# Clustered attention and two MoE layers on one core: first pair's halves placed by engines, arg max head by head, weight chunks loaded from the seventh row block on, 1e-9 added by ACT

## The chip, the core and the metric

One core of a Trainium2 chip runs the whole program. The metric is the device time of one execution in microseconds (us). PE is TensorE, DVE is VectorE, ACT is ScalarE, POOL is GpSimd, and SP is SyncE, which only issues transfers here. "Line 450" or L450 is a line of the kernel as the profile names it.

## What is computed

```python
q_assign = argmax(q_n @ c_n.T)        # 16 clusters for each of 8 heads
k_assign = argmax(k_n @ c_n.T)
mask = q_assign[..., :, None] == k_assign[..., None, :]
scores = where(mask, q @ k.T / sqrt(D), -1e9)
scores = scores - max(scores)
attn = exp(scores)
attn = attn / (sum(attn) + 1e-9)
x = (attn @ v) as [1536, 512]
x = leaky(x @ w_in1) @ w_out1         # d_ff 2048
out = ratio(x @ w_in2) @ w_out2       # ratio of polynomials
```

Batch 2, heads 8, sequence 768, head width 64. All in float32. The weights arrive as 64-bit floats, which the kernel takes as pairs of 32-bit words.

## The kernel before

**Attention.** The 16 (batch, head) slices are taken two at a time as 8 pairs. A pair has 12 row blocks of 128 queries (six for each of its two heads), so there are 96 row blocks, called rows from here on: row 0 is the first, row 12 the first of the second pair. `run` is one loop over rows, and all engines execute what it emits in the order in which it is written. In turn i it emits the row maximum `nm` of row i (DVE), the reciprocal and the scaling of `e` for rows i-2 and i-1 (DVE, POOL), the six transposes `pT` of row i-4 (PE) with their copies `ph` (ACT) and `pl` (DVE), the exponential `e` of row i (ACT), the scores `s` of row i+1 (PE), and matmuls with the values, `o`. So each row follows row by row through PE, DVE, ACT and POOL, four turns deep.

**Float32 in two parts.** PE multiplies in a shorter format, so each operand is split into a high part and the remainder, the low part. For the scores, `a` holds for a head the high part of q over its low part (64 partitions each) and for k the low part over the high part, and `b` holds the high parts once more in its first 64 partitions, with 16 rows of one-hot cluster marks below them. A row's scores are two matmuls with `a` and two with `b`, into one tile `s`.

**Preparing a pair.** q and k are loaded (`load_qk`), transposed on PE into `pa` (`trans`), copied to `x`, split into `hl`, and moved by transfers into `a` and `b` (`place_a`, `place_b`: six transfers of 192 KB a head). For the marks, `sims` multiplies `x` with the centroids, `sims_out` copies the result to `sv`, and DVE and POOL find the first maximum and write the marks `oh` (`sims_max`, `is_max`, `rank`, `first`, `onehot`, called the arg max here); PE transposes them (`onehot_t`), ACT copies them to `ot`, and six small transfers bring them into `b` (`place_oh`). `load_v` and `vsplit` do the values. For pairs 2 to 7 a list, `plan`, says in which turn of the loop each step is emitted. For the first pair and most of the second, `startup` emits everything ahead of row 0.

**Transfers.** Nearly all are issued by SP, in the order of the code, and an issue waits until what it reads is written and what it overwrites is free.

**Weights during attention.** Four chunks of weights (512 KB each) are loaded into tiles `xst` that attention does not need yet, converted in four steps (`conv_a` on ACT, `conv_s` and two `conv_c` on DVE) and saved to DRAM. `weights.step` emits the next of these steps, and `weights.preload` emits loads. Before, two loads are emitted in `startup` ahead of the third pair's q and k, two at its end, and the steps are spread over turns 0 to 53.

**After attention** the two layers run in stages of matmuls with 384 columns (lines 900 on).

Of the kernel before, what the change touches and what calls it, by code (L numbers as in the profile page):

```python
# [17 lines left out]
P = 128  # L18
# [11 lines left out]
def clustered_attention_moe_moe2(  # L30
# [44 lines left out]
    for c in range(C):  # L75
        nc.vector.memset(iom[:, :, c:c + 1], float(c - C))
    lnb = const.tile([P, 1], F32, name="lnb")
# [52 lines left out]
    class Attention:  # L130
# [62 lines left out]
        def prep_pieces(self, p):  # L193
# [9 lines left out]
            def load_qk():  # L203
                for nm in "qk":
                    st[nm] = raw.tile([P, HP, T, D], F32, tag=f"{nm}raw", name=f"{nm}raw")
                for h in range(HP):
# [34 lines left out]
            def split_direct(h, x=True):  # L241
                new_hl(h)
                pps = [st["pp"].pop(("a", h, i)) for i in range(2)]
                if x:
                    st["x"][h] = tok.tile([P, 2, W], F32, tag="x", name="x", bufs=2)
                    for i in range(2):
                        scaled_copy(st["x"][h][:, i], i, pps[i])
                for i in range(2):
                    hi = part(h, 0, i)
                    scaled_copy(hi, i, pps[i])  # L250
                    nc.vector.scalar_tensor_tensor(
                        part(h, 1, i), pps[i], (SCALE, 1.0)[i], f32(hi),
                        op0=ALU.mult, op1=ALU.subtract,
                    )

# [51 lines left out]
            N2 = HP * NS2  # L307

            def svv():
                return st["sv"].rearrange("p h n c -> p (h n) c")  # L310

            def sims_max():
                st["mx"] = sm.tile([P, N2], F32, tag="mx", name="mx")
                nc.vector.reduce_max(st["mx"], svv(), axis=AX.X)

            def is_max():
                nc.vector.tensor_tensor(
                    svv(), svv(), st["mx"].unsqueeze(2).to_broadcast([P, N2, C]), op=ALU.is_ge
                )

            def rank(eng=gp):
                eng.tensor_tensor(svv(), svv(), iom.to_broadcast([P, N2, C]), op=ALU.mult)

            def first():
                nc.vector.tensor_reduce(st["mx"], svv(), axis=AX.X, op=ALU.min)
                st["oh"] = tok.tile([P, 2, HP, T, C], F32R, tag="oh", name="oh")

            def onehot(i):
                mx = st["mx"].rearrange("p (h i t) -> p h i t", h=HP, i=2)
                nc.vector.tensor_tensor(  # L330
                    st["oh"][:, i],
                    iom.unsqueeze(2).to_broadcast([P, HP, T, C]),
                    mx[:, :, i].unsqueeze(3).to_broadcast([P, HP, T, C]),
# [3 lines left out]
            def onehot_t(tile_=self.ptile):  # L337
                pp = tile_("po")
                st["pp"]["o"] = pp
                for i in range(2):  # L340
                    for h in range(HP):
                        j = i * HP + h
                        nc.tensor.transpose(
                            pp[0:C * T, j * P:(j + 1) * P].bitcast(F32R),
# [4 lines left out]
            def onehot_out():  # L349
                pp = st["pp"].pop("o")  # L350
                st["ot"] = tok.tile([P, 2, HP, P], F32R, tag="ot", name="ot")
                w = HP * P
                for i in range(2):
                    nc.scalar.activation(
                        st["ot"][0:C * T, i].rearrange("p h n -> p (h n)"),
                        pp[0:C * T, i * w:(i + 1) * w], AF.Copy, scale=-BIG if i == 0 else 1.0,
                    )

            def place_oh(queues=(nc.sync,)):
                for t in range(T):  # L360
                    queues[t % len(queues)].dma_start(
                        out=f32(st["b"][D:KB, :, :, t % 2 * TH + t // 2, :]),
                        in_=f32(st["ot"][t * C:(t + 1) * C]),
                    )

            def vsplit(h):
# [11 lines left out]
                load_qk, load_v, trans, trans_out, split_direct, split_hi, split_lo, place_a, place_b,  # L378
# [42 lines left out]
            if p == 1:  # L421
# [3 lines left out]
                moved = []  # L425
# [6 lines left out]
            if p == 2:  # L432
                plan = plan[1:]
# [131 lines left out]
        def startup(self, open_start, weights):  # L565
# [3 lines left out]
            self.load_centroids()  # L569
            f0["load_qk"]()  # L570
            load_consts()
            self.centroid_zero()
# [4 lines left out]

            for h in range(HP):
                halves(f0, h)
            f1["load_qk"]()  # L580
            vec.tensor_copy(identr, ident)
            for f in self.centroid_ops():
                f()
            self.centroid_t(po)
            for h in range(HP):
                f0["split_direct"](h)
                f0["place_a"](h, (nc.sync, nc.gpsimd))
                f0["place_b"](h, (nc.sync, nc.gpsimd))
            pq = lambda nm: self.pq.tile([P, 512], F32, tag="pT", name=nm)
            for h in range(HP):  # L590
                f0["sims"](h, pq)
            for h in range(HP):
                f0["sims_out"](h)
            f0["sims_max"]()
            f0["is_max"]()
            f0["rank"](vec)
# [521 lines left out]
```

## Time and profile before

| | |
|---|---|
| median of 3 runs | 841.36 us (840.57 to 842.88) |
| profiled execution, own time | 840.42 us |
| its span | 838.6 us, so 1.8 us lie around it |
| busy share | PE 95%, DVE 77%, ACT 62%, POOL 49% |
| attention, first to last row maximum | 26.55 to 276.0 us |
| transfers | 82.16 MB, mean 98 GB/s |

The busy share is an average over stages: in the two layers PE is busy nearly throughout, in the first 45 us of attention no engine is. What a change at the start is worth is read from the first 60 us, stretch by stretch.

### The profile page before, as it was taken

Reading aid. Unit: us, or ns where it says so; the run is one execution under the profiler, and the core shown is the slowest. Engines: PE = TensorE matmul, PEld = TensorE weight load, DVE = VectorE, ACT = ScalarE, POOL = GpSimd, SP = SyncE. Lnnn points to the kernel's source line nnn. Section 1 sums busy time; section 2 is a strip of 40 time slices with the busy share of each in tenths; the row PEclk is TensorE's granted clock in tenths of the full one; section 3 lists DMA queues with packets and bytes.
Section 4 is the critical chain, followed back from the end, with each engine's and each line's share of the span. In section 5 each row is a group of like instructions: output and inputs, shape, how many; then the busy total and the mean of one; then the engine's idle time right before and its main releaser. Section 6 shows DMA issues by size and latency. Waiting matters only on the chain.

```text
span 838.6 us, 13335 instructions
## 1 busy us (share of the span) xinstructions
PE 796.8 (95%) x4545; PEld 738.5 (88%) x4545; DVE 645.9 (77%) x1221; ACT 520.7 (62%) x1077; POOL 408.7 (49%) x478
## 2 busy tenths in 40 slices
PE   5689999999999899999999999998999999999997
PEld 5588888898888899999999999996889888988995
DVE  4389889889889566857466657768878888888887
ACT  3468788888888544454254345546767667766664
POOL 2676778878756522231022024256555555554442
PEclk9789999999999999999999999999999999999999
DMA  7956637637410214344545453530011110100112
GB/s 182 240 150 159 156 68 154 133 84 150 104 36 26 72 51 179 102 150 140 146 168 176 127 200 105 173 88 26 25 38 26 39 38 26 25 1 1 39 39 75
DMA packets 43987, 82.16 MB, mean 98 GB/s; under 512 B 5488, under 2 KB 26224, under 8 KB 43920
## 3 DMA queue, kind: packets, MB, share of 16 engines
q1 hardware_dynamic: 43296, 80.04, 34.2%
q0 software_dynamic: 384, 1.18, 0.6%
q8 instruction: 36, 0.59, 0.3%
q14 instruction: 31, 0.25, 0.1%
q10 hardware_dynamic: 240, 0.10, 0.1%
HBM read 50.37 MB, written 10.49 MB: 73 GB/s over the span
## 4 chain that ended last, share of the span: by engine, by line
PE 48%; POOL 20%; DVE 11%; ACT 9%; issue 8%; DMA 3%; POOLq 0%; ACTq 0%; SPq 0%; DVEq 0%
PE y L923 19%; PE h L923 19%; POOL z L975 6%; POOL z L972 4%; PE o L525 3%; DVE pl L511 3%; PE pT L492 3%; DVE nm L459 2%; PE s L450 2%; POOL wol L750 2%; ACT ln L988 2%; ACT ph L505 2%; POOL e L484 2%; POOL wil L750 2%; ACT r L989 2%
## 5 line engine op out<-in xcount | busy, mean ns | idle before, releaser
L923 PE MATMUL h<-xh,wil 128*128 128x384 f32 x512 | 172.4, 337 | 0.0
L923 PE MATMUL h<-xh,wih 128*128 128x384 f32 x512 | 172.4, 337 | 0.0
L923 PE MATMUL h<-xl,wih 128*128 128x384 f32 x512 | 172.2, 336 | 0.0
L957 DVE TENSOR_TENSOR gl<-h,gh 128x384 fp32r<-128x384 f32 x128 | 70.9, 554 | 81.2 <-ACT gh L952 64.1
L750 POOL TENSOR_TENSOR wil<-wf,wih 128x512 fp32r<-128x512 f32 x32 | 41.7, 1311 | 146.3 <-ACT wih L747 105.4
L511 DVE TENSOR_TENSOR pl<-pT,ph 128x384 fp32r<-128x384 f32 x192 | 97.1, 547 | 12.6 <-ACT ph L505 11.7
L505 ACT CAST ph<-pT 128x384 fp32r<-128x384 f32 x192 | 83.2, 485 | 33.6 <-PE pT L492 32.7
L484 POOL TENSOR_SCALAR e<-e,sum 128x768 f32<-128x768 f32 x96 | 87.6, 922 | 32.5 <-DVE sum L480 28.4
L459 DVE TENSOR_REDUCE nm<-s 128x1 f32<-128x768 f32 x96 | 91.0, 948 | 14.0 <-PE s L450 13.6
L923 PEld LDWEIGHTS h<-xh,wih 128*128 128x128 f32 x512 | 96.1, 188 | 2.6
L923 PEld LDWEIGHTS h<-xl,wih 128*128 128x128 f32 x512 | 96.0, 188 | 2.5
L470 ACT ACTIVATE e<-s,nm 128x768 f32<-128x768 f32 x96 | 87.5, 911 | 17.0 <-DVE nm L459 11.4
L923 PEld LDWEIGHTS h<-xh,wil 128*128 128x128 f32 x512 | 96.0, 187 | 0.0
L492 PE MATMUL pT<-ident,e 128*128 128x128 f32 x576 | 82.8, 278 | 11.1 <-DVE pl L511 10.8
L961 ACT ACTIVATE h<-h 128x384 f32<-128x384 f32 x64 | 30.5, 476 | 91.3 <-PE h L923 91.2
L952 ACT CAST gh<-h 128x384 fp32r<-128x384 f32 x128 | 61.7, 482 | 40.0 <-DVE h L996 37.5
L923 PE MATMUL y<-gl,woh 128*128 128x384 f32 x256 | 85.6, 334 | 0.2 <-DVE gl L957 0.2
L923 PE MATMUL y<-gh,wol 128*128 128x384 f32 x256 | 85.7, 335 | 0.0
L923 PE MATMUL y<-gh,woh 128*128 128x384 f32 x256 | 85.6, 334 | 0.0
L492 PEld LDWEIGHTS pT<-ident,e 128*128 128x128 f32 x576 | 67.7, 144 | 19.4 <-POOL sum L476 6.1
L972 POOL TENSOR_SCALAR z<-y,abv 128x384 f32<-128x384 f32 x64 | 43.5, 680 | 82.1 <-ACT y L968 82.1
L740 DVE SCALAR_TENSOR_TENSOR wf<-st,wf 128x512 int32<-128x512 int32 x120 | 82.8, 742 | 0.0
(104 smaller groups left out, 1842.1 us busy)
## 6 DMA issues: line engine op xcount, KB each, us to landing
st<-in_moe_w_in_dram SPq DMA_DIRECT2D x30, 512.0 KB, 4.6
st<-in_moe_w_out_dram SPq DMA_DIRECT2D x30, 512.0 KB, 4.5
a<-hl SPq DMA_DIRECT2D x60, 192.0 KB, 4.2
b<-hl SPq DMA_DIRECT2D x30, 192.0 KB, 6.5
wf<-scratch_wi SPq DMA_DIRECT2D x14, 256.0 KB, 3.1
wf<-scratch_wo SPq DMA_DIRECT2D x14, 256.0 KB, 2.9
qraw<-in_q_dram SPq DMA_DIRECT2D x16, 192.0 KB, 3.0
kraw<-in_k_dram SPq DMA_DIRECT2D x16, 192.0 KB, 3.3
```

The source lines that it names most:

```text
L459: nc.vector.reduce_max(un["nm"], un["s"][:, 0:S], axis=AX.X, negate=True)
L470: nc.scalar.activation(un["e"], un["s"][:, 0:S], AF.Exp, bias=un["nm"], accum_out=un["recip"])
L484: nc.gpsimd.tensor_scalar(un["e"], un["e"], un["recip"], 1.0, op0=ALU.mult, op1=ALU.mult)
L492: nc.tensor.transpose(pp[:, kt * P:(kt + 1) * P], un["e"][:, k0:k0 + P], ident)
L505: nc.scalar.copy(un["hi", part], un["pT", part])
L511: nc.vector.tensor_tensor(self.group[gi]["pl"][:, part * n:(part + 1) * n, i * P:(i + 1) * P], un["pT", part], f32(un["hi", part]), op=ALU ...
L740: nc.vector.scalar_tensor_tensor(wi, hold["st", i][:, :, :, 1 - w], sc, wi, op0=op, op1=ALU.bitwise_or)
L750: nc.gpsimd.tensor_tensor(hold["l"][:, i:i + wr, :], hold["wf", i], f32(hold["h"][:, i:i + wr, :]), op=ALU.subtract,)
L923: nc.tensor.matmul(o, lhsT=l, rhs=r, start=(first and idx == 0), stop=(last and idx == n - 1),)
L952: nc.scalar.copy(d["gh"], d["h"])
L957: nc.vector.tensor_tensor(d["gl"], d["h"], f32(d["gh"]), op=ALU.subtract)
L972: nc.gpsimd.tensor_scalar(d["z"], d["y"], abv[:, 1:2], abv[:, 0:1], op0=ALU.mult, op1=ALU.add)
```

## The change

1. In `startup` the first pair's `a` and `b` are no longer filled through `hl` and transfers. `x_out` copies both transposes to `x`; `direct` writes a high part into `a` with ACT and the low part with DVE; `direct_b` copies the high parts from `a` to `b` with POOL. Twelve transfers of 192 KB fall away.
2. The arg max of the first pair is done for each head apart, its marks too, and all its transfers are issued by SP. Before, SP and ACT issued three each.
3. `startup` loads no weights. The first call of `weights.step` is in turn 7 and emits all four loads; steps then come in two turns of three. The last transfers of the second pair's `a` and `b` are emitted in turns -1 and 0. For the third pair, transposes, copies and splits come one turn later.
4. The 1e-9 is added by ACT right behind the exponential of an odd row, and no longer by POOL at the turn's end.

```diff
-            def split_direct(h, x=True):
...
+            def x_out(h):
+                st["x"][h] = tok.tile([P, 2, W], F32, tag="x", name="x", bufs=2)
                 for i in range(2):
+                    scaled_copy(st["x"][h][:, i], i, st["pp"].pop(("a", h, i)))
+
+            def direct(h, i, u):
+                if i == 0 and u == 0:
+                    st["a"][h] = self.tr.tile([P, 2, T, P], F32R, tag="a", name="a", bufs=4)
+                src = st["x"][h][u * D:(u + 1) * D, i]
...
+                nc.scalar.copy(hi, src)
+                nc.vector.tensor_tensor(lo, src, f32(hi), op=ALU.subtract)
+
+            def direct_b(h, i):
...
+                gp.tensor_scalar(
+                    st["b"][0:D, i, h], f32(st["a"][h][i * D:(i + 1) * D, i]),
+                    1.0, 1.0, op0=ALU.mult, op1=ALU.mult,
+                )
...
-            nc.gpsimd.tensor_scalar(un["sum"], un["sum"], 1e-9, 1.0, op0=ALU.add, op1=ALU.mult)
+            nc.scalar.activation(un["sum"], un["sum"], AF.Identity, bias=eps)
...
+            split(0)
+            chain(f0, h0)
+            split(1)
+            assign(h0)
             for h in range(HP):
+                f0["vsplit"](h)
             for h in range(HP):
                 halves(f1, h)
+                by_pool(f1, h)
             f2["load_qk"]()
+            chain(f0, h1)
+            assign(h1)
+            f1["place_a"](0)
...
                     self.exp(i)
+                    if i % 2 == 1:
+                        self.denom(i)
...
-                if i % 2 == 1 and 0 <= i < NU:
-                    self.denom(i - 1)
-                if 0 <= i < NU // 2 + UP // 2:
-                    fill[1].step(2 if i % 3 == 2 else 1)
+                if UP // 2 <= i < NU - 2 * UP and i % 3:
+                    fill[1].step()
```

`split(h)` is two rounds of `direct` and `direct_b`, `chain` is the arg max of one head, `assign` its marks' transposes, copies and transfers, `by_pool` the split of the second pair.

How the instructions stand on the engines. First PE from the first `sims` to the first scores, where `pa` here is the second pair's; before:

```order
L291 MATMUL sims<-cc,x 128x32 x12
L343 MATMUL po<-identr,oh 96x128 x4
L225 MATMUL pa<-ident,qraw 128x128 x3
L225 MATMUL pa<-ident,kraw 128x128 x3
L225 MATMUL pa<-ident,qraw 128x128 x3
L225 MATMUL pa<-ident,kraw 128x128 x3
L450 MATMUL s<-a 128x512
```

and after:

```order
L307 MATMUL sims<-cc,x 128x32 x12
L365 MATMUL po<-identr,oh 96x128 x2
L230 MATMUL pa<-ident,qraw 128x128 x3
L230 MATMUL pa<-ident,kraw 128x128 x3
L230 MATMUL pa<-ident,qraw 128x128 x3
L230 MATMUL pa<-ident,kraw 128x128 x3
L365 MATMUL po<-identr,oh 96x128 x2
L477 MATMUL s<-a 128x512
```

The second head's marks now stand on PE between the second pair's transposes and row 0's scores. Next DVE in `startup`, after the change, up to the first row maximum:

```order
L262 TENSOR_TENSOR a<-x,a 64x384 x4
L335 TENSOR_REDUCE mx<-sv 128x12
L338 TENSOR_TENSOR sv<-sv,mx 128x192
L343 TENSOR_TENSOR sv<-sv,iom 128x192
L346 TENSOR_REDUCE mx<-sv 128x12
L353 TENSOR_TENSOR oh<-iom,mx 128x96 x2
L262 TENSOR_TENSOR a<-x,a 64x384 x4
L335 TENSOR_REDUCE mx<-sv 128x12
L338 TENSOR_TENSOR sv<-sv,mx 128x192
L343 TENSOR_TENSOR sv<-sv,iom 128x192
L346 TENSOR_REDUCE mx<-sv 128x12
L353 TENSOR_TENSOR oh<-iom,mx 128x96 x2
```

Before there were four subtractions (line 251, 384 wide, one input in PSUM) and then one arg max of 384 elements for both heads. Now there are eight subtractions with both inputs in SBUF and two arg maxes of half the width. Last ACT in turns 7 and 8 of the loop, after the change, from the exponential of row 7:

```order
L497 ACTIVATE e,sum<-s,nm 128x768
L503 ACTIVATE sum<-sum,eps 128x2
L767 ACTIVATE xst<-xst 128x512
L532 CAST ph<-pT 128x3x128 x2
L376 ACTIVATE ot<-po 96x256 x2
L497 ACTIVATE e,sum<-s,nm 128x768
L767 ACTIVATE xst<-xst 128x512
```

and SP around the loads that those conversions read:

```order
L220 DMA vraw<-in_v_dram 128x2x384
L286 DMA a<-hl 64x2x384 x4
L755 DMA xst<-in_moe_w_in_dram 128x2x512 x2
L755 DMA xst<-in_moe_w_out_dram 128x1024 x2
L383 DMA b<-ot 16x4x128 x6
```

Before, the conversions (L727) stood behind the exponentials of rows 0 and 1, and their loads ahead of row 0. Now the load and its conversion are emitted in the same turn, and SP has the third pair's first four transfers into `a` ahead of the load.

## Rows read from the trace of the kernel before

**Rows 1.** Stretches: length; busy PE, PEld, DVE, ACT, POOL; clock; DMA share; GB/s.

```profile
26.55:45.19 18.64, 13.53 (x70) 11.83 (x70) 9.66 (x17) 9.35 (x21) 11.12 (x15) 0.68 1.07 264
62.76:95.69 32.93, 31.04 (x211) 27.36 (x209) 31.36 (x58) 26.92 (x62) 23.51 (x31) 1.00 0.54 129
...
127.71:158.77 31.06, 30.14 (x211) 27.40 (x209) 28.00 (x52) 25.62 (x60) 24.60 (x34) 1.00 0.54 118
```

**Rows 2.** Timeline, exponentials of rows 4, 5 and 11: start, length, idle before.

```profile
38.35 0.90 ACT L470 ACTIVATE e<-s,nm 128x768 f32<-128x768 f32 x1 [0.30 <-DVE nm L459]
46.23 0.90 ACT L470 ACTIVATE e<-s,nm 128x768 f32<-128x768 f32 x1 [0.37 <-DVE nm L459]
...
61.59 0.92 ACT L470 ACTIVATE e<-s,nm 128x768 f32<-128x768 f32 x1
```

**Rows 3.** Chain that ended last, 26 to 41 us: start, length, what.

```profile
26.94 7.81 DMA a<-hl
...
39.62 0.83 POOL hl L258
```

**Rows 4.** Timeline of the start, up to row 0's scores.

```profile
6.40 0.85 PE L225 MATMUL pa<-ident,kraw 128*128 128x128 f32 x3
...
8.23 5.30 PE L291 MATMUL sims<-cc,x 128*128 128x32 f32 x24 [0.78 <-DVE cc L186]
14.51 0.56 DVE L317 TENSOR_TENSOR sv<-sv,mx 128x384 f32<-128x384 f32 x1
16.28 0.63 DVE L330 TENSOR_TENSOR oh<-iom,mx 128x192 fp32r<-128x192 f32 x2
...
25.54 0.98 PE L450 MATMUL s<-b 80*128 80x512 f32 x2 [3.77 <-DMA b<-ot]
```

**Rows 5.** Groups by line and form, 127.71 to 220.85 us: busy, mean ns.

```profile
L263 POOL TENSOR_TENSOR hl<-x,hl 128x384 fp32r<-128x384 f32 x12 | 12.0, 1009 | 0.3
L538 ACT COPY tmp<-o 64x384 f32<-64x384 f32 x12 | 5.7, 475 | 1.9 <-PE o L525 1.8
L258 POOL TENSOR_SCALAR hl<-x 128x768 fp32r<-128x768 f32 x6 | 5.0, 838 | 0.0
L476 POOL TENSOR_SCALAR sum<-sum 128x2 f32<-128x2 f32 x18 | 3.5, 192 | 5.9 <-ACT e L470 4.8
```

**Rows 6.** Timeline, DVE beside POOL, at 163 and at 44 us.

```profile
162.69 1.02 POOL L373 TENSOR_TENSOR vs<-vraw,vs 128x384 fp32r<-128x384 f32 x1
163.25 0.88 DVE L317 TENSOR_TENSOR sv<-sv,mx 128x384 f32<-128x384 f32 x1
...
44.13 1.13 DVE L740 SCALAR_TENSOR_TENSOR xst<-xst 128x512 int32<-128x512 int32 x1
44.70 1.43 POOL L263 TENSOR_TENSOR hl<-x,hl 128x384 fp32r<-128x384 f32 x1
```

**Rows 7.** Timeline of SP, a pair's six mark transfers.

```profile
87.71 3.85 SPq L361 DMA_DIRECT2D b<-ot  x6
```

**Rows 8.** DMA issues of the whole span: count, KB each, median us to landing.

```profile
b<-hl SPq DMA_DIRECT2D x30, 192.0 KB, 6.5
...
b<-ot SPq DMA_DIRECT2D x45, 32.0 KB, 2.0
xst<-in_moe_w_in_dram SPq DMA_DIRECT2D x2, 512.0 KB, 4.3
xst<-in_moe_w_out_dram SPq DMA_DIRECT2D x2, 512.0 KB, 7.9
```

**Rows 9.** Timeline: a weight conversion on ACT.

```profile
67.38 0.70 ACT L727 ACTIVATE xst<-xst 128x512 f32<-128x512 f32 x1
```

**Rows 10.** Chain that ended last, three steps of POOL's addition.

```profile
159.76 0.20 POOL sum L476
...
165.30 0.20 POOL sum L476
...
278.80 0.20 POOL sum L476
```

More of the change, by code (lines that the diff above doesn't have):

```diff
@@ L201, in prep_pieces, with load_qk @@
             W = TH * P
[L203 to L206, printed above, removed]
+            ALL = (0, HP)
+            def load_qk(hs=ALL):
+                if hs[0] == 0:
+                    for nm in "qk":
+                        st[nm] = raw.tile([P, HP, T, D], F32, tag=f"{nm}raw", name=f"{nm}raw")
+                for h in range(*hs):
                     for nm, src in (("q", q), ("k", k)):
@@ L319, in is_max, with rank @@
                 )
[L321 to L329, printed above, removed]
+            def rank(hs=ALL, eng=gp):
+                eng.tensor_tensor(svv(hs), svv(hs), iom.to_broadcast(wide(hs)), op=ALU.mult)
@@ L424, in prep_pieces @@
                 done = ("load_qk", "trans", "trans_out", "split_hi", "split_lo", "place_a", "place_b")
-                moved = []
+                moved = [
+                    (-13, "end", place_b, 0),
+                    (-12, "end", place_a, 1),
+                    (-12, "end", place_b, 1),
+                ]
                 for x, slot, f, *a in plan:
@@ L432, in prep_pieces @@
             if p == 2:
-                plan = plan[1:]
+                late = ("trans", "trans_out", "split_hi", "split_lo")
+                plan = [(x + (f.__name__ in late), slot, f, *a) for x, slot, f, *a in plan[1:]]
             return [(p * UP + x, slot, lambda f=f, a=a: f(*a)) for x, slot, f, *a in plan]
@@ L576, in halves, with by_pool, chain @@
                     f["trans"](h, i, pp=t[:, i * 512:i * 512 + BLK])
+            def by_pool(f, h):
+                f["trans_out"](h, 0)
+                f["trans_out"](h, 1)
+                f["split_hi"](h)
+                f["split_lo"](h, 0)
+                f["split_lo"](h, 1)
+            def chain(f, hs):
+                f["sims_out"](hs[0])
+                f["sims_max"](hs)
+                f["is_max"](hs)
+                f["rank"](hs, vec)
+                f["first"](hs)
+                f["onehot"](0, hs)
+                f["onehot"](1, hs)
@@ L578, in startup @@
+            self.load_centroids()
+            f0["load_qk"](h0)
+            f0["load_qk"](h1)
+            load_consts()
+            self.centroid_zero()
+            vec.tensor_copy(identr, ident)
+            open_start()
+            for f in self.centroid_ops():
+                f()
             for h in range(HP):
                 halves(f0, h)
[L580 to L583, printed above, removed]
             self.centroid_t(po)
@@ L585, in startup @@
             for h in range(HP):
[L586 to L589, printed above, removed]
-            for h in range(HP):
[L591 to L596, printed above, removed]
-            f0["first"]()
@@ L598, in startup, with split @@
-            for i in range(2):
-                f0["onehot"](i)
-            f0["onehot_t"]()
-            f0["onehot_out"]()
-            f0["place_oh"]((nc.sync, nc.scalar))
-            f0["load_v"]()
-            open_start(2)
+                f0["x_out"](h)
+                f0["sims"](h, pq)
+            f1["load_qk"]()
+            f0["load_v"]()
+            def split(h):
+                for i in range(2):
+                    for u in range(2):
+                        f0["direct"](h, i, u)
+                    f0["direct_b"](h, i)
@@ L611, in startup @@
-                f1["split_lo"](h, 1)
-            weights.slow = True
-            f2["load_qk"]()
-            f0["vsplit"](0)
-            f0["vsplit"](1)
-            for h in range(HP):
-                f1["place_a"](h)
-                f1["place_b"](h)
-            weights.preload(len(weights.wst))
+                by_pool(f1, h)
+            f2["load_qk"]()
+            chain(f0, h1)
+            assign(h1)
+            f1["place_a"](0)
         def run(self, extra, fill):
@@ L873, in open_start @@
                 queue_scratch(0)
-                weights.preload(n)
         def open_weights(which, par, **kw):
```

100 lines of the change are left out of this document (52 added, 48 removed).

## The prediction

> **What bounds the kernel now.** The stretches come first, cut at the starts of row maxima (26.55 is row 0, 45.19 row 5, 62.76 row 12, 95.69 row 24). From 127.71 on, 12 rows take 31.06 us and PE is busy for 30.14 of them [rows 1]: 2.59 a row, PE-bound, with 0.92 us of PE idle a pair. Ahead of that two stretches are longer. Five rows from 26.55 to 45.19 took 18.64 us at a mean granted clock of 0.68 (partly 1.2 and partly 2.4 GHz, PE idle for 5.1 us of them) and a DMA share over 1 [rows 1]. The twelve rows from 62.76, which contain the conversions of two weight chunks, took 32.93, 1.87 more than a settled pair [rows 1].
>
> Then the exponentials, for where the first stretch lost its time: row 4's is at 38.35, row 5's at 46.23 [rows 2]. 7.88 for one row is 5.3 too many. The chain that ended last names the cause: transfers `a<-hl` of the second pair from 26.94, then POOL's split of the third pair at 39.62, which reuses the buffer that they read [rows 3]. POOL's queue is in order, so the scaling of rows 2 and 3 stood behind that split. Ahead of row 0 the chain is the marks: `s<-b` of row 0 starts at 25.54 after waiting 3.77 us for `b<-ot` [rows 4].
>
> The two layers after attention are PE-bound and not touched; I let them move rigidly with the end of attention.
>
> **The change, step by step. Step 1, row 0's scores.** Through `sims` nothing moves: 8.23 to 13.53 for both heads, so head 0's half is done at 10.9 [rows 4]. The last transposes of the first pair end at 7.25 (6.40 + 0.85 [rows 4]); ACT's copy to `x`, 0.45, ends at 7.7. ACT then writes head 0's four high parts at about 0.45 each (a 64 x 384 copy is 0.475 [rows 5]), ready at 8.2, 8.6, 9.1 and 9.5.
>
> DVE's subtractions are the unknown. Alone a 384-wide operation with two SBUF inputs takes 0.56 [rows 4]. But beside POOL it took 0.88: it was issued at 163.25, POOL's operation ended at 163.71, and it ended 0.42 later [rows 6]. The other way round, POOL's 1.01 us subtraction took 1.43 when DVE was at work as it was issued [rows 5, 6]. So the two take turns, whole operations at a time, and a waiting 384-wide DVE operation costs 0.42 after POOL lets go. On this I let them alternate: `direct_b` (0.74 held; 768 wide, 0.84 alone [rows 5]) between the subtractions; head 0's four end at 11.7 instead of 10.6; its arg max (six operations of half width, 1.9 alone by halving [rows 4]) meets POOL's `direct_b` of head 1 and the first `vsplit` and ends at 14.85 instead of 13.25. PE 0.45, ACT 0.55, six transfers in 3.85 [rows 7] and 2.0 to land [rows 8] give 21.75 for head 0's marks.
>
> These are not last, though. The second head's marks stand on PE ahead of row 0's scores (the order shown above). Head 1's subtractions alternate with `vsplit` and end at 19.4; its arg max alternates with POOL's splits (1.01 and 0.84 [rows 5]) and ends at 23.5; two transposes (0.45) and the first part of row 0's scores (0.65) give `s<-b` at 24.7. Against 25.54 that is **-0.8**. The ends: with no waiting the same additions give 20.7 (-4.8); with every operation charged in full after each wait, 28.2 (+2.7).
>
> The Trainium skill's page "SBUF — State Buffer", section "Who interferes with whom", says that a DVE instruction with two SBUF inputs and a GpSimd instruction that reads SBUF exclude one another for the whole instruction, and that one with at most one SBUF input doesn't contend. Rows 6 agree for the arg max; no trace here shows the 64 x 384 subtraction, which the rule would include, and whose predecessor read PSUM. By the rule the start is 24.7, by the old subtraction's freedom nearer 20.7.
>
> **Step 2, rows 1 to 11.** I moved row 0 to 24.7 and went through the queues with the durations of before. The second pair's transfers now begin behind head 1's marks, at 28.5, without 1 MB of weights and without the first pair's 2.3 MB; head 0's six land near 35. POOL reaches the third pair's split near 36.5, so it doesn't wait: the **5.3** goes. Two things are late next. Load and conversion of a weight chunk share turn 7. SP issues the load after the third pair's four transfers, which wait for POOL's split: near 44, and it lands 4.3 later [rows 8], near 48.2. ACT, in order, is behind row 7's exponential near 46.2 and waits **2.0** there; `ph` of row 4 and all later copies and exponentials stand behind it. Two conversions of 0.70 [rows 9], which lay in idle time of ACT in rows 0 and 1, now lie where ACT is behind: **1.4**. Together -1.9. The end on the good side is -5.3, if the load is early. On the other side the landing takes 7.9, as the other load did [rows 8]: 3.6 more.
>
> The marks of the second pair are issued behind 2 MB of loads. SP's four loads are in by 53, the marks issued near 50.5 to 54.5 land by 56.5, and row 12 needs them near 59. I cost this at nothing; without that cover each us late is a us of delay.
>
> **Step 3, the spread weights.** The 1.87 over a settled pair was for eight conversion operations within seven rows. Now the first two chunks' DVE operations lie in turns 10 to 17, the others in 34 to 44, thinner. I take 0.8 and 1.0 against 1.87: **0**, between -1.1 (half hidden) and +1.9 (both cost in full).
>
> **Step 4, the 1e-9.** POOL's addition is 0.19 [rows 5] and stands on the chain twice a pair behind POOL's splits, as at 159.76 and 165.30, and once more at 278.80 near the end [rows 10]. Each occurrence goes with about 0.1 of hand-over: 0.6 a pair. ACT gets one small operation every other row. No row shows it; between nothing and the 0.2 of POOL's I take 0.2, and one of six a pair on the path: 0.2 back. So 0.4 a pair over seven pairs, and 0.3 at the end: **-3.1**. The ends are 0 and all of PE's idle time, 0.92 times seven, -6.4.
>
> **Sum.** -0.8 - 1.9 + 0 - 3.1 = -5.8 against the profiled 840.4: 834.6. The median of the runs shown is 0.9 above that execution, so 835.5 in its terms.
>
> **Rivals**, from 835.5.
> - *DVE and POOL hardly meet* at the start, since POOL's splits wait for `x` more often than I think. For it: one meeting costs only what is left of the other's operation. Against it: POOL has 12 us of such work there. Four less: 831.5.
> - *They meet in full*: 28.2 instead of 24.7, 839.0, no change.
> - *The POOL wait returns*: the six transfers take 6.5 or more from the last issue (median of `b<-hl` [rows 8]), land behind POOL's split, and rows 2 and 3 wait again. For it: my margin is 1.5 us. Up to 5.3 more: 840.8, nothing won.
> - *The weight load is later*, 7.9 instead of 4.3: 839.1.
> - *Slower: ACT becomes the path.* All 48 small operations delay `ph` and the next exponential by 0.2 and a hand-over of 0.04: 11.5, and 3.1 isn't won: 850.1. For it: each stands directly ahead of `ph`, which PE's transposes wait on. Against it: ACT is busy for 25.62 of 31.06 us [rows 1], and 1.2 more still leaves 4. It decides for slower from 5.3 us on, if 22 of the 48 are on the path.
>
> **Chances.** Forecast 0.44, hardly meet 0.24, meet in full 0.10, POOL wait 0.09, late load 0.06, ACT 0.07. This kernel's measurement tells some 0.3% (2.5 us) from no change: faster is below 838.8. That takes the first two and a little of the third and fifth, 0.72; slower is ACT's alone, 0.07; the rest, 0.21, is the same. The range runs from the second case with part of step 4's upper end, 829, to the POOL wait's, 841. The likeliest case alone runs from 832 to 838.5.
>
> **What the profile would show.** Step 1: row 0's `s<-b` near 24.7, released by ACT or PE and not by DMA; the subtractions (line 262) at 0.56 when POOL is idle and up to 1.2 beside it. A start below 22 means that they hardly meet, above 27 that they meet in full. Step 2: no gap of 5 us between two exponentials of rows 0 to 6, and one of about 2 us ahead of the first conversion (line 767). Step 3: the twelve rows from row 12 under 32.9 us, those from row 36 over 31.06. Step 4: DVE's reciprocal no longer waits behind POOL, settled pairs near 30.7 us; above 31.06 ACT is the path. The forecast is wrong if the layers after attention don't move with its end, or if the clock stays low longer than before: 18.64 us of the first five rows were at 0.68 [rows 1], and I left the early rows' matmuls at their length of before.

## The result and the profile after

The changed kernel took 832.2 us (median of 5 runs, 831.5 to 833.51) against 841.11 for the kernel before (5 runs, 839.64 to 842.88): ratio 0.9899, 95% interval [0.9882, 0.9917]. The forecast was 835.5 and faster. The profiled execution took 831.54 us with a span of 829.7, against 840.42 and 838.6.

Where the 8.9 us of span come from is read from the starts of the row maxima. Row 0 starts at 24.52 instead of 26.55 (-2.03). From row 0 to row 12 the loop takes 34.28 instead of 36.21 (-1.93), from row 12 to row 95 209.87 instead of 213.22 (-3.35), and from row 95 to the end of the span 561.0 instead of 562.6 (-1.6). The stretches of the kernel after, cut at rows 0, 5, 12, 24, 36, 48 and, the last, 60 and 72 (columns as in [rows 1]):

```profile
24.52:36.86 12.34, 12.15 (x66) 10.86 (x65) 7.35 (x12) 7.64 (x19) 4.00 (x5) 0.71 0.72 154
36.86:58.80 21.94, 17.66 (x126) 15.62 (x124) 15.78 (x31) 16.79 (x42) 13.38 (x15) 1.00 0.80 214
58.80:90.83 32.03, 29.90 (x206) 26.86 (x205) 30.65 (x56) 27.14 (x66) 23.03 (x26) 1.00 0.54 117
90.83:121.57 30.74, 29.91 (x210) 27.50 (x209) 28.00 (x53) 27.62 (x68) 23.35 (x28) 1.00 0.59 142
121.57:153.89 32.32, 30.96 (x211) 27.57 (x210) 31.44 (x58) 28.18 (x68) 23.95 (x27) 1.00 0.53 117
...
184.53:215.26 30.73, 29.89 (x210) 27.48 (x209) 27.96 (x52) 27.07 (x67) 23.44 (x28) 1.00 0.54 117
```

The first five rows, 18.64 us in [rows 1], take 12.34, and PE is busy for 12.15 of them: hardly a wait is left there, and for over half of the time PE ran at 1.2 GHz (mean granted clock 0.71). The next seven took 17.57 before (row 12's 62.76 less row 5's 45.19) and take 21.94, with PE idle for 4.3 of them. A settled pair takes 30.73 instead of 31.03.

The start, which answers to [rows 4], in the timeline of the kernel after (start, length, engine, line, what, idle before and what ended it):

```profile
8.50 3.33 DVE L262 TENSOR_TENSOR a<-x,a 64x384 fp32r<-64x384 f32 x4 [0.49 <-ACT a L261]
9.10 2.33 POOL L267 TENSOR_SCALAR b<-a 64x768 fp32r<-64x768 f32 x2 [7.58 <-ACT a L261]
...
13.93 0.65 DVE L353 TENSOR_TENSOR oh<-iom,mx 128x96 fp32r<-128x96 f32 x2
...
14.61 4.06 DVE L262 TENSOR_TENSOR a<-x,a 64x384 fp32r<-64x384 f32 x4
19.88 0.35 DVE L335 TENSOR_REDUCE mx<-sv 128x12 f32<-128x192 f32 x1 [1.21 <-ACT sv L318]
...
20.69 1.03 DVE L343 TENSOR_TENSOR sv<-sv,iom 128x192 f32<-128x192 f32 x1
...
22.14 0.54 DVE L353 TENSOR_TENSOR oh<-iom,mx 128x96 fp32r<-128x96 f32 x2
...
22.66 0.42 PE L365 MATMUL po<-identr,oh 128*96 128x128 f32 x2 [5.10 <-DVE oh L353]
...
22.87 0.97 PE L477 MATMUL s<-a 128*128 128x512 f32 x2
...
23.64 0.84 PE L477 MATMUL s<-b 80*128 80x512 f32 x2
...
24.52 0.96 DVE L486 TENSOR_REDUCE nm<-s 128x1 f32<-128x768 f32 x1 [1.84 <-PE s L477]
```

`s<-b` of row 0 waits for no transfer. The wait that ends last is now 5.10 us of PE for the second head's arg max. The eight subtractions (L262) stand in two groups and take 0.83 and 1.02 us each on average.

Two waits of rows 4 to 8, in the same view, where [rows 2] had 7.88 us between two exponentials:

```profile
35.63 0.83 POOL L274 TENSOR_SCALAR hl<-x 128x768 fp32r<-128x768 f32 x1
35.70 0.91 ACT L497 ACTIVATE e<-s,nm 128x768 f32<-128x768 f32 x1
...
37.91 0.90 ACT L497 ACTIVATE e<-s,nm 128x768 f32<-128x768 f32 x1
...
48.52 0.66 ACT L767 ACTIVATE xst<-xst 128x512 f32<-128x512 f32 x1 [3.44 <-DMA xst<-in_moe_w_in_dram]
```

POOL's split of the third pair no longer waits for the second pair's transfers, and the exponentials of rows 4 and 5 are 2.21 apart. In its place ACT waits 3.44 us for the first weight chunk.

Last the groups by line and form over attention (busy, mean ns of one, idle just before and what ended it), of the kernel before:

```profile
L480 DVE RECIPROCAL sum<-sum 128x2 f32<-128x2 f32 x48 | 7.6, 159 | 13.8 <-POOL sum L476 13.5
```

and after:

```profile
L503 ACT ACTIVATE sum<-sum,eps 128x2 f32<-128x2 f32 x48 | 14.2, 296 | 1.6
L507 DVE RECIPROCAL sum<-sum 128x2 f32<-128x2 f32 x48 | 7.4, 154 | 0.8 <-ACT sum L503 0.5
```

DVE's waiting ahead of the reciprocal falls from 13.8 us to 0.8, although the addition itself takes 0.30 on ACT against 0.19 on POOL [rows 5]. A third of the 13.8 is one wait in the first five rows of the kernel before. There POOL's addition stood behind the split of the third pair at 39.62 [rows 3], so the wait that step 2 of the prediction is about reached DVE through the addition of step 4:

```profile
42.67 0.17 DVE L480 RECIPROCAL sum<-sum 128x2 f32<-128x2 f32 x1 [4.35 <-POOL sum L476]
```

### The profile page after: what moved, and what is told of

Read it like the earlier page. It is cut to its first block, busy times and chain, and to the rows that moved or that the text cites. A ratio compares the mean times of both kernels' runs of the same rounds, so it can differ in the third digit from the quotient of the medians.

```text
span 829.7 us, 13350 instructions
## 1 busy us (share of the span) xinstructions
PE 793.6 (96%) x4545; PEld 736.9 (89%) x4545; DVE 653.8 (79%) x1232; ACT 534.3 (64%) x1131; POOL 400.7 (48%) x428
## 4 chain that ended last, share of the span: by engine, by line
PE 51%; POOL 16%; DVE 13%; ACT 9%; issue 8%; DMA 1%; SPq 1%; POOLq 0%; DVEq 0%; ACTq 0%
PE y L961 19%; PE h L961 19%; POOL z L1013 6%; PE o L552 4%; POOL z L1010 4%; PE pT L519 4%; DVE pl L538 3%; PE s L477 3%; DVE nm L486 3%; ACT ln L1026 2%; POOL wol L790 2%; ACT r L1027 2%; PE sims L307 2%; POOL wil L790 2%; ACT ph L532 1%
## 5 line engine op out<-in xcount | busy, mean ns | idle before, releaser
L519 PE MATMUL pT<-ident,e 128*128 128x128 f32 x576 | 80.7, 275 | 5.3 <-DVE pl L538 5.3
L961 PE MATMUL y<-woh,gh 128*128 128x512 f32 x192 | 76.6, 399 | 4.7 <-ACT gh L990 3.8
```

What stands on the lines that cost most here:

```text
L519: nc.tensor.transpose(pp[:, kt * P:(kt + 1) * P], un["e"][:, k0:k0 + P], ident)
L961: nc.tensor.matmul(o, lhsT=l, rhs=r, start=(first and idx == 0), stop=(last and idx == n - 1),)
```

## The experiments

Twelve kernels, each compared with the kernel before. The table gives the ratio with its interval, the start of row 0's maximum and the lengths of stretches between the maxima of the rows named (differences of their starts in the timeline, one execution each). Twelve rows, a pair's worth, are called a dozen.

| kernel | median | ratio | row 0 | 0-5 | 5-12 | 12-24 | 24-36 | 36-48 | 48-60 | 60-72 | 72-95 |
|---|---|---|---|---|---|---|---|---|---|---|---|
| before | 841.11 | 1 | 26.55 | 18.64 | 17.57 | 32.93 | 32.02 | 31.06 | 31.05 | 31.03 | 55.13 |
| after | 832.2 | 0.9899 [0.9882, 0.9917] | 24.52 | 12.34 | 21.94 | 32.03 | 30.74 | 32.32 | 30.64 | 30.73 | 53.41 |
| e1 | 836.6 | 0.994 [0.9924, 0.9956] | 26.89 | 16.71 | 19.45 | 33.40 | 30.76 | 30.76 | 30.76 | 30.70 | 53.44 |
| e2 | 841.25 | 0.999 [0.9979, 1.0001] | 26.74 | 15.35 | 19.61 | 32.49 | 31.46 | 33.49 | 32.02 | 31.02 | 55.14 |
| e3 | 840.07 | 0.9993 [0.9974, 1.0011] | 33.03 | 14.13 | 20.28 | 31.55 | 30.76 | 32.38 | 30.63 | 30.74 | 53.67 |
| e4 | 839.1 | 0.9972 [0.9961, 0.9984] | 24.82 | 14.67 | 20.61 | 32.51 | 31.53 | 33.52 | 32.07 | 31.02 | 55.18 |
| e5 | 830.96 | 0.9889 [0.9866, 0.9912] | 24.70 | 14.14 | 19.38 | 32.00 | 30.80 | 32.33 | 30.60 | 30.73 | 53.39 |
| e6 | 832.71 | 0.991 [0.9891, 0.9928] | 25.42 | 14.14 | 20.28 | 32.03 | 30.75 | 32.31 | 30.62 | 30.78 | 53.41 |
| e7 | 830.99 | 0.9903 [0.9878, 0.9929] | 22.81 | 14.67 | 20.93 | 32.02 | 30.76 | 32.31 | 30.62 | 30.72 | 53.41 |
| e8 | 834.94 | 0.9936 [0.9917, 0.9955] | 25.48 | 13.46 | 24.30 | 32.30 | 30.74 | 30.75 | 30.72 | 30.73 | 53.40 |
| e9 | 832.72 | 0.9913 [0.9891, 0.9936] | 24.73 | 14.14 | 20.63 | 32.06 | 30.55 | 32.43 | 30.40 | 30.54 | 53.48 |
| e10 | 834.19 | 0.9934 [0.991, 0.9959] | 27.68 | 13.08 | 25.48 | 31.52 | 30.76 | 32.36 | 30.56 | 30.71 | 53.46 |
| e11 | 839.66 | 0.9981 [0.9967, 0.9994] | 24.73 | 20.77 | 17.94 | 32.95 | 32.03 | 31.07 | 31.06 | 31.04 | 55.12 |
| e12 | 830.26 | 0.9863 [0.9844, 0.9883] | 24.45 | 14.67 | 20.34 | 32.05 | 30.58 | 32.36 | 30.44 | 30.54 | 53.42 |

### Part 4, the addition: e1, e4, e9

e1 is the kernel before with part 4 alone, e4 the changed kernel without it.

```diff
 e1, to the kernel before:
-            nc.gpsimd.tensor_scalar(un["sum"], un["sum"], 1e-9, 1.0, op0=ALU.add, op1=ALU.mult)
+            nc.scalar.activation(un["sum"], un["sum"], AF.Identity, bias=eps)
...
                     self.exp(i)
+                    if i % 2 == 1:
+                        self.denom(i)
```

> The kernel before with only the 1e-9 moved to ACT. If POOL's addition stood on the path (step 4): a settled pair of 12 rows falls from 31.05 us to about 30.7, the rows from 72 on lose about 2 us together, the whole 4 to 5 us: 836.5. Rival: PE bounds the rows anyway and the addition is hidden: 841, a settled pair stays at 31.05. Second rival: ACT's 0.30 us delays the copies: pairs above 31.05, 845.

> The change with the 1e-9 back on POOL at the turn's end. If step 4 is worth what the traces of before and after differ by from row 12 on: 836 to 837, a settled pair at 31.05 again. Rival: 832 to 833, nothing changes.

e1's ratio is 0.994: by itself part 4 gives 5.0 us (3.7 to 6.4). e4's is 0.9972: taking it out of the changed kernel loses 6.1 (0.0073 of 841), more than the difference of the traces had let expect (836 to 837; the median is 839.1). The columns of the table say where. A settled pair gives 0.3 (31.03 to 30.70), rows 24 to 36 give 1.26, rows 72 to 95 1.7. In e4, rows 36 to 60 together take 65.59 against 62.96 in the changed kernel, 2.6 more. The dozen from row 24 explains the uneven size. Here is the kernel before, POOL and then DVE in the timeline:

```profile
95.13 1.01 POOL L373 TENSOR_TENSOR vs<-vraw,vs 128x384 fp32r<-128x384 f32 x1
96.10 0.52 POOL L560 TENSOR_SCALAR xh<-xf 128x384 fp32r<-128x384 f32 x1
96.70 1.01 POOL L561 TENSOR_TENSOR xl<-xf,xh 128x384 fp32r<-128x384 f32 x1
97.80 0.19 POOL L476 TENSOR_SCALAR sum<-sum 128x2 f32<-128x2 f32 x1
...
98.02 0.17 DVE L480 RECIPROCAL sum<-sum 128x2 f32<-128x2 f32 x1 [1.38 <-POOL sum L476]
```

and e1 at the same place:

```profile
97.32 0.15 DVE L482 RECIPROCAL sum<-sum 128x2 f32<-128x2 f32 x1
97.39 1.00 DVE L513 TENSOR_TENSOR pl<-pT,ph 128x384 fp32r<-128x384 f32 x2
```

Before, the 0.19 us addition stood behind the splits of v and of the output; DVE's reciprocal waited 1.38 for it, and in DVE's queue the subtractions for `pl` stood behind the reciprocal. In e1 DVE goes on at once.

e9 leaves the addition out of the changed kernel.

```diff
-                    if i % 2 == 1:
-                        self.denom(i)
```

> The changed kernel without the addition of 1e-9 (a part of the computation left out; a row's sum holds the exponential of 0, about 1, which float32 leaves as it is when 1e-9 is added). Theory (ScalarE's 48 small operations of 0.30 us are nearly all beside the path, the gain of part 4 was that GpSimd no longer adds): settled dozens stay near 30.7 us, time 831.5 to 832.2. Rival (the prediction's estimate of 0.2 us back on the path in a pair): dozens at 30.5, time near 830.6. Second rival (all 48 delay the copies behind them): 14 us less, below 820.

Settled pairs take 30.54 instead of 30.73, 0.19 less, as the rival had it for a pair, and the time is not measurably different (0.9913 against 0.9899, the intervals overlap). So ACT's 48 operations cost little, and what part 4 gave is that DVE no longer waits for POOL's queue. The edit changes two things at once, though: the engine, and the place in the code, which is now right behind the exponential and no longer behind the turn's splits. POOL adding at the new place wasn't run, so how much the place alone gives is not shown.

### Part 3, the weights: e2, e8, e5

e2 is the kernel before with the loads and steps of part 3, e8 the changed kernel with those of before.

```diff
 e8, to the changed kernel:
+            weights.preload(2)
...
+            weights.preload(4)
...
-                if UP // 2 <= i < NU - 2 * UP and i % 3:
-                    fill[1].step()
+                if 0 <= i < NU // 2 + UP // 2:
+                    fill[1].step(2 if i % 3 == 2 else 1)
```

> The kernel before with only the weight loads and steps emitted as in the change (first in turn 7). If the 1 MB of loads ahead of the second pair's transfers caused POOL's wait at 39.6: the wait is gone or under 0.5 us and row 5's maximum starts near 41 instead of 45.2, but ACT then waits 3 us or more for the first weight load in turn 7: 839 to 841. Rival: the first pair's own 2.3 MB cause it: row 5 stays at 44 to 45 and the late load comes on top, 843 to 845.

> The changed kernel, with the weight chunks loaded in the startup and converted from row block 0 on, as the kernel before does; all other parts stay. Theory (as the run of the kernel before with this part alone gave 841.25 against 841.11, the two shifts of it cancel: the early rows pay POOL's wait, the rows from 36 to 60 gain 2): 832 to 833.5, with row 9 earlier or later by under 2 us and the rows from 36 to 60 at 30.7 a dozen. Rival (in the new order POOL's and SP's queues are short of room, so the early load costs in full): the first rows pay the 6.6 us that POOL waited for the first chunk, time 836 to 838. Second rival (the early rows now wait for nothing on POOL, so spreading is a pure loss): 830.

In the kernel before, part 3 gives nothing that can be told (0.999). Its first expectation came true for the most part in the trace: POOL's idle time ahead of the third pair's first split is 1.16 us (it was 4.15), and row 5 starts at 42.09 instead of 45.19. So the weight loads caused most of that wait, not the first pair's own transfers, which e2 keeps. ACT's wait for the first chunk, 2.02, is under the 3 that were expected. In sum the first 12 rows win 1.25 (36.21 to 34.96), rows 12 to 36 win 1.0, and rows 36 to 60 lose 3.4 (62.11 to 65.51). In the changed kernel it is needed: e8's first 12 rows take 37.76 against 34.28, because POOL's wait for transfers is back, in its timeline just ahead of row 6:

```profile
42.14 0.84 POOL L274 TENSOR_SCALAR hl<-x 128x768 fp32r<-128x768 f32 x1 [5.15 <-DMA a<-hl]
```

The expectation that the two shifts cancel (832 to 833.5) fell, and the rival that the early load costs in full (836 to 838) did too: 834.94, a ratio of 0.9936 against 0.9899, 3.1 us, with intervals that touch. Of that, 0.96 in the profiled execution is another thing: row 0 itself started later, since the first pair's q and k landed later, which no weight load precedes (e11, with the same loads, has row 0 at 24.73). And the spread costs rows 36 to 60 less once ACT adds: 62.96 against 61.47, 1.5 instead of 3.4.

e5 issues the first weight load at the end of turn 2 instead of in turn 7.

```diff
                 go("end")
+                if i == 2:
+                    fill[1].preload(4)
```

> The changed kernel, with the first weight chunk's transfer issued at the end of row block 2 and its conversions left where they are. Theory (ScalarE's 3.44 us wait ahead of the first conversion is on the path, as the changed kernel's trace has the maxima of rows 8 and 9 6.3 us apart where settled rows are 2.6 apart): the wait goes and row 9's maximum starts near 47.5 instead of 50.5, for a time near 829.5. Rival (the wait lies in time that the front of row blocks 0 to 12 loses anyway, to the second and third pairs' work on VectorE): row 9 starts earlier but row 12 is still at about 58.8, time 832. Second rival: the load at row 2 holds up the third pair's q and k behind it, 833 to 835.

ACT's wait is gone and row 9 starts at 49.23 instead of 50.52, not at 47.5. Row 12 gains 0.6 on the profiled execution of the changed kernel and 1.3 on e9, whose loop starts alike. The time is not measurably lower (0.9889 against 0.9899). So 3.44 us of waiting were worth about 1.

### Parts 1 and 2, the start: e3, e11, e6, e7

e3 brings back the splits into `hl` and the twelve transfers for the first pair and keeps all else. e11 is the changed kernel without part 4 and without the loads and steps of part 3. It keeps parts 1 and 2, and also what part 3 does to the second and third pairs' turns.

```diff
 e3, to the changed kernel:
-                f0["x_out"](h)
+                f0["split_direct"](h)
+                f0["place_a"](h, (nc.sync, nc.gpsimd))
+                f0["place_b"](h, (nc.sync, nc.gpsimd))
...
-                for i in range(2):
-                    for u in range(2):
-                        f0["direct"](h, i, u)
-                    f0["direct_b"](h, i)
+                pass
```

> The change with the first pair's halves again split in the old way and moved by transfers; the arg max stays head by head. If the transfers held row 0 back: its scores with b wait for b<-ot again and its maximum starts at 26 or later instead of 24.5, and POOL waits for the second pair's transfers (rows 5 later by 2 to 4): 835 to 837. Rival: the second head's arg max sets row 0's start whatever places the halves, and without the subtractions beside POOL it even ends earlier: row 0 at 23 to 24.5, 831 to 832.

> The changed kernel with parts 1 and 2 alone: weights loaded and converted as before, 1e-9 added by GpSimd. Theory of sums (832.2 and the 2.9 that the weights and the 6.9 that the addition are worth in the changed kernel): 842, so the start alone gains nothing, row 0 is about 1 us earlier than in the kernel before but the first dozen of rows takes longer as the weights are converted in it. Rival (the 2 us by which row 0 comes earlier stay): 839.

e3's row 0 starts at 33.03, 6.5 later than before the change and far behind both expectations; the time, 840.07, is that of the kernel before. Its chain that ended last:

```profile
15.48 1.60 SPq L301
...
17.17 6.64 DMA qraw<-in_q_dram
...
23.95 2.81 PE pa L230 x12
...
27.95 0.36 DVE mx L350
...
31.50 2.55 PE s L492 x7
```

SP issues the second pair's q and k behind the first pair's transfers. In ACT's queue the copy `sv`, which the second head's arg max reads, now stands behind the copies of the second pair's transposes, so row 0 waits for those loads. In the new order, placing by engines is worth 8.5 us at row 0. What it is worth in the old order wasn't run.

e11 shows what the start is worth without the rest: 0.9981 [0.9967, 0.9994], 1.6 us. Row 0 starts 1.8 earlier, as in the changed kernel, but the first 12 rows take 38.71, 2.5 more than before, with the same wait as in e8:

```profile
41.83 0.83 POOL L274 TENSOR_SCALAR hl<-x 128x768 fp32r<-128x768 f32 x1 [4.71 <-DMA a<-hl]
```

So the start gives 1.8 and takes back 2.5 as long as weights are loaded in it; the spans of the two profiled executions differ by 0.3 (838.3 and 838.6). The median stood nearer to the rival's 839 than to the sum's 842.

e6 computes the low parts from PSUM instead of from the copy `x`, so that one operand lies in SBUF instead of two.

```diff
-                nc.vector.tensor_tensor(lo, src, f32(hi), op=ALU.subtract)
+                nc.vector.scalar_tensor_tensor(
+                    lo, st["pp"]["a", h, i][u * D:(u + 1) * D], (SCALE, 1.0)[i], f32(hi),
+                    op0=ALU.mult, op1=ALU.subtract,
+                )
```

> The changed kernel, with the first pair's low parts computed from PSUM (one operand in SBUF, scaled in the same instruction) instead of from the copy x (two operands in SBUF). Theory (VectorE's and GpSimd's operations on SBUF take turns there: the two subtractions that ran beside GpSimd's copies took over 0.8 each, those alone 0.56): the eight subtractions take 0.6 each, VectorE's arg max starts up to 1 us earlier, row 0's maximum near 23.7, time near 831.4. Rival (the arithmetic from PSUM costs as much as the turns did, or ScalarE's copies of the high part set the pace): row 0 stays at 24.5, time 832.2. Second rival: PSUM buffers held longer delay the second pair's transposes, row 0 after 25, time over 833.

In e6's timeline of the start:

```profile
8.66 2.31 DVE L262 SCALAR_TENSOR_TENSOR a<-pa,a 64x384 fp32r<-64x384 f32 x4 [0.49 <-ACT a L261]
...
13.70 2.31 DVE L262 SCALAR_TENSOR_TENSOR a<-pa,a 64x384 fp32r<-64x384 f32 x4
...
16.39 0.90 PE L230 MATMUL pa<-ident,qraw 128*128 128x128 f32 x3 [1.03 <-ACT x L233]
...
19.15 0.35 DVE L338 TENSOR_REDUCE mx<-sv 128x12 f32<-128x192 f32 x1 [3.13 <-ACT sv L321]
19.54 1.19 DVE L341 TENSOR_TENSOR sv<-sv,mx 128x192 f32<-128x192 f32 x1
...
22.05 1.53 DVE L356 TENSOR_TENSOR oh<-iom,mx 128x96 fp32r<-128x96 f32 x2
```

All eight subtractions take 0.58 each beside the same copies of POOL, so the two SBUF inputs were what made them 0.83 and 1.02. The Trainium skill's page "SBUF — State Buffer", section "Who interferes with whom", says that a DVE instruction with at most one SBUF input, outside the two-port modes, doesn't contend with GpSimd; this trace agrees for the 64 x 384 subtraction, at 0.58. But DVE then waits 3.13 for ACT's copy `sv`, and the arg max of the second head, four of whose six operations still have two SBUF inputs, meets POOL's splits instead: 1.19 for an operation that took 0.36 for the first head, and 4.4 for the whole arg max against 2.8 in the changed kernel. Row 0 starts 0.9 later. The taking of turns was moved, not won. The second rival may have a share in it. PE's transposes for the second pair begin 0.9 earlier than in the changed kernel, but the later half of them waits 1.03 us, as it would if buffers in PSUM were held longer, and ends 0.4 later; ACT's copy `sv` stands behind the copies of these transposes. How much of the 0.9 that is, no run shows.

e7 emits the second head's arg max and marks behind row block 0's scores.

```diff
-            chain(f0, h1)
-            assign(h1)
-            f1["place_a"](0)
+            self.late = (
+                lambda: chain(f0, h1), lambda: assign(h1), lambda: f1["place_a"](0),
+            )
...
+                if i == first:
+                    for f in self.late:
+                        f()
```

> The changed kernel, with the second head's arg max, its marks' transposes and copies and the second pair's first transfers written behind row block 0's scores instead of ahead of them. Theory (TensorE reaches row 0's scores only behind the second head's mark transposes, which wait 5.10 for VectorE's arg max; row 0 is of the first head and needs none of it): row 0's scores start at about 21, its maximum at about 22.7 instead of 24.5, and half or more of that stays to the end, time 830.4 to 831.3. Rival (row 0's maximum on VectorE still stands behind the arg max, or the marks come too late for the rows of the second head): row 0 or row 5 gains nothing, time 832 to 833.

Row 0 starts at 22.81 as the theory had it. Beside e9, in whose trace PE's matmuls took the long form about as long as here (to 38 or 39 us), it starts 1.9 earlier, row 5 1.4 earlier (37.48 against 38.87) and row 12 1.1 (58.41 against 59.50). What was lost went to PE: it is busy for all of the 14.67 us of the first five rows.

```profile
22.81:37.48 14.67, 14.67 (x60) 13.69 (x61) 7.53 (x12) 8.15 (x20) 6.63 (x8) 0.50 0.70 160
```

The granted clock is 0.50, so 1.2 GHz, throughout. The time, 0.9903, can't be told from the changed kernel's.

### Parts 3 and 4 together, and three edits on top: e10, e12

e10 is e1 with the edit of e2. e12 is the changed kernel with the edits of e5, e7 and e9.

> The kernel before with parts 3 and 4 of the change and without parts 1 and 2. Theory of sums (part 4 alone gave 4.9 us and part 3 alone nothing): 836 to 836.5. Rival (the two help each other, as in the changed kernel the spread weights are worth 2.9 us and the addition 6.9): the dozen of rows from 36 that takes 33.5 us when GpSimd adds falls to about 32.3, time 833 to 835, and parts 1 and 2 are then worth only 1 to 3 us at the end.

> The changed kernel with the first weight load three row blocks earlier, the second head's marks behind row block 0's scores, and no addition of 1e-9 (left out; see the run without it alone). Theory (each of the first two gave about 1.2 us in the median and they touch different places, the third gives little): row 0's maximum near 22.8, row 12's near 57.7, time 829 to 830. Rival (both edits fill the same slack ahead of row 12): row 12 near 58.3, time 831.

e10's ratio, 0.9934 [0.991, 0.9959], is 5.5 us with 3.4 and 7.6 as its bounds, which holds the sum of e1 and e2 (5.0 and 0.8) and the rival alike; the median, 834.19, lies in the rival's 833 to 835. The dozen from row 36 did fall from 33.49 in e2 to 32.36, as the rival had it. Its executions lie between 833.18 and 840.05, and the profiled one, 839.05, is among the longest, so its second stretch of 25.48 isn't that of the median.

e12 has the lowest ratio, 0.9863, against 0.9899 for the changed kernel; the intervals [0.9844, 0.9883] and [0.9882, 0.9917] barely meet. Row 12 starts at 59.46, no earlier than in e9, so the profiled execution doesn't show the two early edits adding up. It is the longest of the five (831.91, median 830.26), and PE's clock fell in it once more: the two matmuls with `a` at 45.47 took 0.99, after 0.60 at 41.57. Row 0, at 24.45, didn't keep e7's 22.81, though PE was faster there: the first products with the centroids took 3.10 us instead of e7's 5.30, head 1's copies to `b` on POOL followed head 0's at once, and both arg maxes met POOL more often. In DVE's timeline of e12 their marks are longer:

```profile
14.39 1.23 DVE L351 TENSOR_TENSOR oh<-iom,mx 128x96 fp32r<-128x96 f32 x2
...
22.89 1.53 DVE L351 TENSOR_TENSOR oh<-iom,mx 128x96 fp32r<-128x96 f32 x2
```

In e7 they take 0.66 and 0.54. Between these two traces, how DVE and POOL fall against one another makes up the 1.6 us at row 0, and the faster PE ahead of it didn't help.

## Right and wrong, by the prediction's steps

**Direction and mechanisms.** Faster was forecast with 0.72, and the time lies inside the range and 3.3 below the forecast, at the lower edge of what the likeliest case alone was to give (832 to 838.5). Of the 8.9 us, 5.8 were in the sum; the other 3.1 are sizes that the steps had wrong and a part behind attention whose cause is open.

**Step 1** was -0.8 and measured -2.0 (-1.9 by `s<-b`). The mechanism held: no transfer releases row 0's scores, and the second head's marks are last. Head 0's subtractions ended at 11.83 (11.7 forecast) and its arg max at 14.58 (14.85). The term that was too large is the second head's: its subtractions ended at 18.67 instead of 19.4, and its arg max took 2.8 instead of 4.1, as fewer of its operations met POOL. It gained less than that, because it first waited 1.21 for ACT's copy `sv`, which the step didn't have, and ended at 22.68 instead of 23.5. The taking of turns was real (e6), and `s<-b` at 23.64 lies between the signs for "hardly meet" (under 22) and "meet in full" (over 27). That the old subtraction's freedom would bring row 0's start near 20.7 didn't come true: e6 has that freedom, and its `s<-b` starts at 24.54, as its arg max still meets POOL. Two sums of the step are off by a little without effect: the terms given add up to 21.70, not 21.75, for head 0's marks, and to 24.6, not 24.7, for `s<-b`.

**Step 2** was -1.9 and measured -1.9 for rows 0 to 12, but not by its parts, and that the sum agrees is in part luck. The wait of POOL went, as forecast, and e2, e8 and e11 show that the late weights are what keeps it away; without the first pair's transfers but with early weights, e11's POOL waits 4.71 (the rival "the POOL wait returns" comes true without the late weights). ACT waited 3.44 for the weights instead of 2.0, though e5 shows that only about 1 of it counted. And in the profiled execution the clock rose early (below): e6 and e9, which have the same rows, took 14.14 for the first five instead of 12.34, and 34.42 and 34.77 for rows 0 to 12, so -1.8 and -1.4. What the step held fixed, and the prediction named as a risk, is the clock: in the kernel before, PE stood idle for 4.78 us because of POOL's wait, and the scores behind it took 0.99 instead of the 0.59 ahead of it.

```profile
36.84 0.59 PE L450 MATMUL s<-a 128*128 128x512 f32 x2
...
43.44 1.51 PE L492 MATMUL pT<-ident,e 128*128 128x128 f32 x6 [4.78 <-DVE pl L511]
44.60 0.99 PE L450 MATMUL s<-a 128*128 128x512 f32 x2
```

**Step 3** was 0 between -1.1 and +1.9. In rows 12 to 60 the spread weights cost 1.2 with ACT adding (e8's 124.51 against 125.73) and 2.5, past the upper end, with POOL adding (e11's 127.11 against e4's 129.63). The signs forecast for it were right: the dozen from row 12 at 32.03, under 32.9, and the one from row 36 at 32.32, over 31.06.

**Step 4** was -3.1 and mis-sized. Alone it is worth 5.0 and beside the spread weights 6.1. The settled pairs came as forecast (30.7; ACT's share 0.19 for 0.2). What failed is to take the settled pair's 0.4 seven times. The addition's price is the queue ahead of it on POOL: 1.38 of waiting in the dozen of row 24, 1.7 us over rows 72 to 95, where one wait is 1.86, and 2.6 in rows 36 to 60, where the weights' steps load DVE. The row of DVE's waits for POOL's addition, 13.5 us over all of attention, was there to be cut by stretches; the prediction read only the addition's steps on the chain. The whole row would have been too much, as 4.35 of it belongs to step 2, and a settled pair has 0.8 of it (0.27 and 0.54) and gained 0.3.

**The sum by place**: row 0 missed 1.2, rows 12 to 95 0.5 (-2.8 forecast from steps 3 and 4, -3.35 measured), and the part behind row 95 1.3 (-0.3 forecast, -1.6 measured). Of the last, 0.4 lies ahead of the first layer, whose first matmul starts 11.78 us behind row 95's maximum before and 11.40 after. The rest is spread over the two layers, which no part of the change touches. From row 95 to the end of the span the kernels here took between 560.8 and 562.6, those with the addition on POOL from 561.6 to 562.6 and the others up to 561.7, so the cause of this part is open.

**Rivals.** ACT did not become the path (e9). The POOL wait did not return, with late weights. The late load came true in part and was mostly absorbed. That parts help each other is left open: the parts apart give 5.0 (e1), 0.8 (e2, an interval that holds 0) and 1.6 (e11), 7.4 in sum, the whole 8.5 (7.0 to 9.9). The traces show two such links, POOL's wait that needs part 3, and the conversions that cost less with part 4, but the times can't prove them.

## What to carry to other kernels

A tiny operation in an in-order queue costs what stands ahead of it, and that differs from stretch to stretch: read the waits of the engine that it releases stretch by stretch, not one settled period times a count. Two edits that only look independent belong together: here the new order of issue lost all that the change gave as long as transfers moved the first pair's halves (e3). Test such edits apart and together. A wait that is removed is worth what the rows behind it move, which was about a third of its length here (e5).

## What the hardware showed that was not expected

The clock of the first rows decides more than most waits, and it can differ where the work is the same. In the changed kernel PE's matmuls take their long form until about 31 us and the short one from 33.08 on. In e5 they take the long one until past 38, although PE's work up to 31 us is the same there, 0.2 later.

The kernel after, timeline of PE:

```profile
29.90 0.99 PE L477 MATMUL s<-a 128*128 128x512 f32 x2
...
33.08 0.59 PE L477 MATMUL s<-a 128*128 128x512 f32 x2
```

e5, timeline of PE, and the stretch over the same rows:

```profile
37.01 0.99 PE L477 MATMUL s<-a 128*128 128x512 f32 x2
...
39.69 0.60 PE L477 MATMUL s<-a 128*128 128x512 f32 x2
```

```profile
24.70:38.84 14.14, 14.14 (x58) 13.17 (x58) 7.54 (x13) 7.71 (x18) 4.84 (x6) 1.00 0.75 161
```

The granted clock of e5's stretch reads 1.00, while its matmuls take the 0.99 us that go with 0.50 in e7's stretch. Early in a trace the lengths of matmuls tell which of 1.2 and 2.4 GHz it was, and the clock's row doesn't always. It can also fall later: in e10's profiled execution it did so after ACT had waited 3.98 us for the weights and PE had stood idle for 3.6, and four rows took 18.77 us.

```profile
47.47:66.24 18.77, 15.14 (x79) 14.20 (x78) 9.55 (x20) 10.69 (x28) 6.06 (x8) 0.73 0.70 206
```

After the changed kernel's wait of 3.44, with PE idle for 3.08, it didn't fall. In e12 it fell with no such wait: PE had stood idle for only 0.71 just before. What decides it is not shown by these runs.
